# Selection rows by engine copies, normalisation also on POOL, halved last stores and more K transposes by DMA in an attention and gated-MLP kernel

## The chip, the cores and the metric

The kernel runs on one core of a Trainium2 chip. A core has five engines with an instruction stream each: TensorE (PE), VectorE (DVE), ScalarE (ACT), GpSimd (POOL) and SyncE (SP), which here only issues transfers. 16 DMA engines move data between HBM and the on-chip memory SBUF. TensorE writes its results to PSUM. The metric is the device time of one execution in microseconds (us); a smaller one is better.

## The reference

```
q, k, v: 4 batches x 8 heads x 768 positions x 64, float32
k_min, k_max = minimum and maximum of k over each chunk of 32 positions (24 chunks)
ub    = sum over d of max(q*k_min, q*k_max)          # a bound per query and chunk
top   = the 6 chunks with the largest bound, among those not after the query's
attn  = softmax(q k^T / 8, over keys in the top chunks and not after the query)
x     = attn v, heads side by side: 4 x 768 x 512
h     = gelu_tanh(x w_in);  u, g = halves of h (512 columns each)
g_n   = (g - mean) / sqrt(var + 1e-6) * g_ln
g_s   = w_sg g_n + b_sg                               # mixes the 768 positions
out   = x + (u * g_s) w_out
```

## The kernel before

*Units.* Two heads make a pair; there are 16 pairs `p`, four to a batch `b`. A pair goes through preparation, scores, and the product with v; after four pairs the MLP of that batch runs. A tag such as `sc_8_1_0` names one piece of work: the scores of pair 8, head 1, piece 0.

*Preparation.* q and k come in as rows and are transposed. For q (`qside`) TensorE transposes in float32 (`qtr`, L524), ScalarE or VectorE take the result out of PSUM (`qev`, L435/L438), a bf16 copy goes to the tile QA (`qcast`), and a copy without its negative part to rT (`rel`). For K there are two ways. Pairs below KD (`kside`): TensorE transposes (`ktr`, L524), VectorE takes minima and maxima by chunk (`kmm`, L563), evictions write the tile KA (`kev`). Pairs from KD on (`kside_full`): VectorE reduces k rows with a transposing reduction (`kred`, L580), TensorE puts the results in order (`perm`, L602) and VectorE copies them (`wcp`); a bf16 copy of k (`kcast`) is transposed into KA by a DMA transpose that SyncE issues (`kT`, L587). KD is 12.

*Selection.* TensorE forms the bounds (`ub`, L662 or L709); VectorE transposes them in blocks (`utr`), finds the sixth largest (`m8`), compares (`dn`) and transposes back (`dt`) into the tile Dt. From pair 4 on two pairs are selected together, and four transfers per two pairs (`qd`, L742, issued by SyncE) copy the rows of Dt into spare partitions of QA, 32 partitions by 576 columns each. The matching spare partitions of KA hold an indicator of chunks, so that one product over 128 partitions gives the score and a large negative number where the chunk was not selected.

*Scores and heads.* TensorE forms scores (`sc`, L778, and L818/L824 for pairs 0 to 3); ScalarE takes the exponential (`exp`, L784, L833); POOL clears what lies above the diagonal (`aff`, L789, L840). The product with v (`pv`, L856, and `pvd`, L863) also gives the sum; VectorE divides (`rcp`, `xs`, L871/L873) into XS.

*MLP of a batch.* XS is transposed, for batches 1 and 2 by DMA transposes (`dt_x`, L882), else on TensorE (`xtr`). Then `hv` (L905), its gelu (`gv`, L909) and statistics (`bns`, `bna`), the inverse root by a power on POOL (`rstd`, L920), and the normalisation of six row blocks (`vhat`, VectorE at L933 or ScalarE at L928). `hu` (L945) is the other half with its gelu (`gu`). `pt` (L962) mixes positions, VectorE multiplies (`vs`, `gt`), `ou` (L981) is the last product, VectorE adds x (`os`, L988) into one of three buffers osb, and SyncE stores it (`st`, L992).

*Order.* Nothing is scheduled at run time. The program builds a list of operations with their dependences; a table written into the kernel gives, for each engine, the order of its operations, the PSUM slot of each tile, an engine for operations that may run on several (`engine`), and the number of matmuls without use ahead of an operation of TensorE (`filler`). Each engine waits on semaphores for what its next instruction needs, and everything behind it in its order waits too. Before, 9 of 156 SyncE operations in the table's order are shown here, from the part in which batch 1's MLP begins:

```
kn_12 st_0_4 kn_11_0 kn_10_0 dt_x_1_0 dt_x_1_1 qd_8_1 dt_x_1_2 dt_x_1_3
```

Of the kernel before, what the change touches and what calls it, by code (L numbers as in the profile page):

```python
# [6 lines left out]
ALU = mybir.AluOpType  # L7
# [225 lines left out]
def dve(n, over=70, rate=1.0):  # L233
    o = n / rate / 0.96 + over
    return o, o + 83
# [22 lines left out]
def dmac(issue=530):  # L258
    return issue, issue


def _build(nc, ctx, q, k, v, w_in, g_ln, w_sg, b_sg, w_out, out):
# [49 lines left out]
    KD = 12  # L312
# [181 lines left out]
    QRUN = [0] * 16  # L494
    KRUN = [0] * 16
# [80 lines left out]
    def kside_full(p, u, x):  # L576
# [7 lines left out]
        for i in range(2):  # L584
            flex("pool", ("act",), lambda i=i: kbx[n][:, i, :, 64 * i:64 * i + 64], lambda i=i: kn[s][:, i], TG + 60,
                 ("kcast", p, i), [("kn", s, 0), ("kn", s, 1), ("kbi", n, i)], [("kbx", n, i)])
            P.op("sp", lambda e, i=i: e.dma_start_transpose(  # L587
                KA[w][i][:].rearrange("p (t x) -> p t x", x=128), kbx[n][:, i].rearrange("p t c -> p (t c)")), dmac(1250),
                ("kT", p, i), reads=[("kbx", n, i), ("kbi", n, i)], writes=[("KA", w, i, 0), ("KA", w, i, 1), ("KI", w, i)],
                dma=f"kT{w}_{i}", xfer=900)  # L590
# [102 lines left out]
    def select_full(pairs, u, v_):  # L693
# [45 lines left out]
        for x, p in enumerate(pairs):  # L739
            for i in range(2):  # L740
                w, g0 = p % NW, 32 * (2 * (1 - i) + x)
                P.op("sp", lambda e, w=w, i=i, g0=g0: e.dma_start(  # L742
                    QA[w][i][g0:g0 + 32, LO:S], Dt[v_][g0:g0 + 32].rearrange("p a b -> p (a b)")), dmac(590),
                    ("qd", p, i), reads=[("Dt", v_)], writes=[("QD", w, i)], dma=f"qd{w}_{i}", xfer=150)
# [133 lines left out]
    def xtrans(b, dk):  # L878
        src = XS[:, b % 2, dk]
        rd = [("XS", b % 2, 2 * dk), ("XS", b % 2, 2 * dk + 1)]  # L880
        if (b, dk) in DXT:
            P.op("sp", lambda e: e.dma_start_transpose(xT[b % 2][:, dk, :].rearrange("p (t x) -> p t x", x=128),  # L882
# [13 lines left out]
    def moe_h(b):  # L896
# [28 lines left out]
        for qt in range(NT):  # L925
# [6 lines left out]
            else:  # L932
                o = P.op("dve", lambda d, qt=qt: d.tensor_scalar(vhat[s][:, qt, :], vg[qt], mv[s][:, qt, 0:1],  # L933
                                                                 rstd[s][:, qt:qt + 1], op0=ALU.subtract,
                                                                 op1=ALU.mult),
                         (456, 548), ("vhat", b, qt), port=True,
                         reads=[("vg", qt), ("mv", s, qt), ("nmr", s), ("rstd", s)], writes=[("vhat", s, qt)])
            o.alts = {"act": (704, 809), "dve": (456, 548)}
# [15 lines left out]
    def moe_g(b):  # L954
        s = b % 2
        for tg in range(2):
# [19 lines left out]
            for qt in range(3 * tg, 3 * tg + 3):  # L976
                t = ps_g.tile((2, 3) if b < B - 1 else None)

                def ou(e, t=t, qt=qt):
# [7 lines left out]
                os_ = (b * NT + qt) % 3  # L987
                P.op("dve", lambda d, t=t, qt=qt, os_=os_: d.tensor_tensor(  # L988
                    osb[os_][:].rearrange("p (a x) -> p a x", x=128),
                    t.ap()[:, 0:DM].rearrange("p (a x) -> p a x", x=128), XS[:, b % 2, :, qt, :], op=ALU.add), dve(DM), ("os", b, qt),  # L990
                    reads=[t] + [("XS", b % 2, hh) for hh in range(H)], writes=[("osb", os_)], ps=[t])
                P.op("sp", lambda e, qt=qt, os_=os_: e.dma_start(  # L992
                    bass.AP(out.tensor, (b * S + 128 * qt) * DM, [[DM, 128], [1, DM]]), osb[os_][:]), dmac(),
                    ("st", b, qt), reads=[("osb", os_)], dma=f"o{os_}", xfer=680)
# [52 lines left out]
    for p in range(4, NP + 4):  # L1047
# [37 lines left out]
    "act": (  # L1085
# [10 lines left out]
    "dve": (  # L1096
# [106 lines left out]
```

## Time and profile before

| | |
|---|---|
| three runs | 219.81 us median, 219.38 to 221.41 |
| profiled execution | 220.97 us, span 219.1 us, mean granted TensorE clock 0.982 |
| busy | PE 205.8, DVE 185.9, ACT 169.5, POOL 93.2 us |
| DMA | 35.48 MB in 95067 packets, 162 GB/s mean |
| 24 `qd` transfers | 36 KB each, landing after a median 2.6 us |

The span is the time from the first to the last instruction of the trace. An engine is busy while it has an instruction in work; matmuls overlap, and a busy TensorE need not be at its peak. The granted clock is the share of TensorE's full clock. A row of a group of instructions names line, engine, operation, output and inputs, shapes and count, then the busy time in us, the mean ns of one, and the idle time of its engine just before with what ended it. A row of the chain of waits or of the timeline begins with its start and its length in us. PEld is TensorE's weight load, and SPq the issue of a transfer by SyncE.

### The profile page before, as it was taken

How to read it: one execution, taken by the hardware profiler on the slowest of the kernel's cores; microseconds unless marked ns; L12 is line 12 of the kernel's file. 1: busy time of each engine (PE TensorE's matmuls, PEld its weight loads, DVE VectorE, ACT ScalarE, POOL GpSimd, SP SyncE). 2: the span in 40 equal slices, each digit the busy share in tenths (PEclk: the TensorE clock that was granted, in tenths of full speed). 3: DMA queues.
4: the chain of work that ended last, by engine and by line, in shares of the span. 5: the costliest groups of instructions: out<-in, count | busy, mean ns of one | idle time of the engine just before them, and what ended most of it. 6: DMA issues, size and time to landing. Idle time of an engine off the chain costs nothing.

```text
span 219.1 us, 5967 instructions
## 1 busy us (share of the span) xinstructions
PE 205.8 (94%) x2357; PEld 134.1 (61%) x2357; DVE 185.9 (85%) x536; ACT 169.5 (77%) x256; POOL 93.2 (43%) x130
## 2 busy tenths in 40 slices
PE   7799999999999999997998989998799999999991
PEld 3477777846767577783355666776545669545640
DVE  3889999799999999998799987985896876968982
ACT  3778999979899899998668888998768978575000
POOL 8434699894374556464023537185102414002000
PEclk9879999999999999998899999999999999999999
DMA  7999999993999988947999849642955004000325
GB/s 153 249 219 205 223 211 375 294 237 124 248 225 238 208 231 200 225 81 135 263 233 179 141 81 224 75 113 56 217 105 124 0 0 146 3 0 0 144 87 201
DMA packets 95067, 35.48 MB, mean 162 GB/s; under 512 B 89280, under 2 KB 90048, under 8 KB 95040
## 3 DMA queue, kind: packets, MB, share of 16 engines
q1 hardware_dynamic: 95040, 35.11, 72.6%
q8 instruction: 18, 0.29, 0.6%
q14 instruction: 9, 0.07, 0.1%
HBM read 24.77 MB, written 6.29 MB: 142 GB/s over the span
## 4 chain that ended last, share of the span: by engine, by line
PE 63%; DVE 16%; ACT 11%; DMA 4%; issue 3%; SPq 0%; DVEq 0%
PE PSG L962 11%; PE PSG L945 7%; PE PSG L905 7%; PE PSC L778 7%; PE PSG L524 6%; ACT E L784 5%; PE PSG L856 4%; PE PSG L981 4%; DMA QA<-Dt 4%; DVE osb L988 3%; PE PSG L709 3%; PE PSC L818 3%; PE PSG L662 3%; DVE Wall L563 2%; DVE U L718 2%
## 5 line engine op out<-in xcount | busy, mean ns | idle before, releaser
L784 ACT ACTIVATE E<-PSC 128x1024 bf16<-128x1024 f32 (+1 forms) x72 | 63.4, 916 | 8.2 <-PE PSC L778 7.0
L778 PE MATMUL PSC<-QA,KA 128*128 128x128 bf16 (+2 forms) x336 | 37.2, 246 | 2.2 <-ACT E L784 1.2
L962 PE MATMUL PSG<-wsgT,vhat 128*128 128x384 bf16 x192 | 35.3, 326 | 0.6 <-DVE vhat L933 0.6
L789 POOL TENSOR_SCALAR_AFFINE_SELECT E<-E 128x768 bf16<-128x768 bf16 x24 | 21.1, 885 | 30.6 <-ACT E L784 30.2
L778 PEld LDWEIGHTS PSC<-QA,KA 128*128 128x128 bf16 x336 | 24.3, 98 | 12.6 <-ACT E L784 3.2
L438 POOL CAST QA<-qT 64x768 bf16<-64x768 f32 (+1 forms) x24 | 20.6, 860 | 22.1 <-ACT qT L435 13.4
L905 PE MATMUL PSG<-winb,xT 128*128 128x512 bf16 x96 | 24.4, 397 | 1.8 <-DVE XS L873 1.1
L962 PEld LDWEIGHTS PSG<-wsgT,vhat 128*128 128x128 bf16 x192 | 17.8, 98 | 11.8 <-ACT qT L435 1.0
L563 DVE TENSOR_REDUCE Wall<-PSG 128x12 f32<-128x384 f32 x48 | 24.7, 540 | 0.3 <-PE PSG L524 0.2
L945 PE MATMUL PSG<-xT,winb 128*128 128x384 bf16 x128 | 24.4, 327 | 0.0
L950 ACT ACTIVATE uT<-PSG 128x384 bf16<-128x384 f32 x32 | 15.5, 490 | 11.3 <-PE PSG L945 10.6
L981 PE MATMUL PSG<-woutb,uT 128*128 128x512 bf16 x96 | 23.7, 379 | 0.0
L909 ACT ACTIVATE vgb<-PSG 128x512 f32<-128x512 f32 x24 | 14.3, 598 | 11.0 <-PE PSG L905 10.9
L968 DVE SCALAR_TENSOR_TENSOR PSG<-PSG,glnT,bsgbc 128x384 f32<-128x384 f32 x32 | 19.5, 618 | 2.4 <-PE PSG L962 2.3
L920 POOL TENSOR_TENSOR rstd<-rstd,neghalf 128x6 f32<-128x6 f32 x4 | 5.3, 1330 | 37.5 <-DVE rstd L918 37.5
L833 ACT ACTIVATE E<-PSC 128x1024 bf16<-128x1024 f32 (+1 forms) x24 | 20.7, 918 | 0.2
L856 PE MATMUL PSG<-vx,E 128*128 128x65 bf16 x480 | 19.9, 194 | 0.4 <-DVE osb L988 0.3
L988 DVE TENSOR_TENSOR osb<-PSG,XS 128x512 f32<-128x512 f32 x24 | 16.0, 683 | 5.0 <-PE PSG L981 4.0
L914 DVE BATCH_NORM_STATS2 stats<-vgb 128x6 f32<-128x512 f32 x24 | 16.2, 681 | 3.2 <-ACT vgb L909 3.0
L856 PEld LDWEIGHTS PSG<-vx,E 128*128 128x128 bf16 x480 | 17.3, 98 | 2.3 <-DVE osb L988 0.6
L873 DVE TENSOR_TENSOR XS<-PSG,rden 128x384 bf16<-128x384 f32 x32 | 17.6, 554 | 0.6
L972 DVE TENSOR_TENSOR uT<-PSG,uT 128x384 bf16<-128x384 f32 x32 | 17.3, 550 | 0.5
(106 smaller groups left out, 370.8 us busy)
## 6 DMA issues: line engine op xcount, KB each, us to landing
qn<-in_q_dram SPq DMA_DIRECT2D x32, 192.0 KB, 4.5
vn<-in_v_dram SPq DMA_DIRECT2D x16, 384.0 KB, 5.5
out_dram<-osb SPq DMA_DIRECT2D x24, 256.0 KB, 2.7
kn<-in_k_dram SPq DMA_DIRECT2D x24, 192.0 KB, 4.6
uT<-in_moe_w_sg_dram SPq DMA_DIRECT2D x4, 384.0 KB, 5.8
vgb<-in_moe_w_in_dram SPq DMA_DIRECT2D x3, 512.0 KB, 9.1
kn<-in_k_dram SPq DMA_DIRECT2D x4, 384.0 KB, 4.5
QA<-Dt SPq DMA_DIRECT2D x24, 36.0 KB, 2.6
```

The lines of the kernel that those rows point to most:

```text
L438: return e.tensor_copy(dst(), src())
L563: P.op("dve", lambda d, m=m, op=op, t=t, hf=hf: d.tensor_reduce(W[w][:, m, 12 * hf:12 * hf + 12], t.ap()[:, 0:TG].rearrange("p (c x) -> p ...
L778: r = e.matmul(t.ap()[:, o:o + n], KA[w][i][:, 128 * kb:128 * kb + 128], QA[w][i][:, q0:q0 + n], start=True, stop=True)
L784: P.op("act", lambda e, t=t, c0=c0, c1=c1, i=i: e.activation(E[es][:, i, c0:c1], t.ap()[:, 0:c1 - c0], ACTF.Exp, scale=SCALE), act(c1 - c0 ...
L789: P.op("pool", lambda g, ev=ev: g.affine_select(ev, ev, pattern=[[0, NT], [1, 128]], compare_op=ALU.is_ge, fill=0.0, base=0, channel_multi ...
L833: P.op("act", lambda e, t=t, c0=c0, c1=c1, n=n: e.activation(E[es][:, :, c0:c1], t.ap().rearrange("p (i x) -> p i x", i=2)[:, :, 0:n], ACT ...
L856: r = e.matmul(t.ap()[:, 65 * qb:65 * qb + 65], E[es][:, i, a:a + 128], vx[w][:, kb, i, :], start=first, stop=False, skip_group_check=True)
L905: r = e.matmul(t.ap()[:, 0:F], xT[s][:, dk, 128 * qt:128 * qt + 128], winb[:, dk, F:DFF], start=(dk == 0), stop=(dk == NDK - 1))
L945: r = e.matmul(t.ap()[:, 0:TG], winb[:, dk, 128 * fb:128 * fb + 128], xT[s][:, dk, TG * tg:TG * tg + TG], start=(dk == 0), stop=(dk == NDK ...
L962: r = e.matmul(t.ap()[:, 0:TG], vhat[s][:, sb, 128 * fb:128 * fb + 128], wsgT[:, sb, TG * tg:TG * tg + TG], start=(sb == 0), stop=(sb == N ...
L981: r = e.matmul(t.ap()[:, 0:DM], gT[s][:, fb, 128 * qt:128 * qt + 128], woutb[:, fb, :], start=(fb == 0), stop=(fb == NF - 1))
L988: P.op("dve", lambda d, t=t, qt=qt, os_=os_: d.tensor_tensor(osb[os_][:].rearrange("p (a x) -> p a x", x=128), t.ap()[:, 0:DM].rearrange(" ...
```

## The change

1. KD goes from 12 to 10: pairs 10 and 11 take the second way for K.
2. The `qd` copies become operations that the table may give to POOL, VectorE or ScalarE: 16, 4 and 4. They are marked `shift`, by which POOL waits for the instruction before it on POOL and the next one waits for it.
3. `vhat` may also run on POOL. By batch, POOL takes 4, 5, 0 and 1, VectorE 0, 0, 6 and 4, ScalarE 2, 1, 0 and 1.
4. The last three row blocks of the output are added and stored in halves, into the q buffers instead of osb; their stores may be issued by ScalarE (three of six are).
5. DMA transposes may be issued by another engine by the table; here all stay on SyncE.
6. The table is new: all five orders, the slots, the fillers (12 matmuls at three places; before, 8 at one) and the engines of other operations.

```diff
-    KD = 12
+    KD = 10
...
-                P.op("sp", lambda e, w=w, i=i, g0=g0: e.dma_start(
-                    QA[w][i][g0:g0 + 32, LO:S], Dt[v_][g0:g0 + 32].rearrange("p a b -> p (a b)")), dmac(590),
-                    ("qd", p, i), reads=[("Dt", v_)], writes=[("QD", w, i)], dma=f"qd{w}_{i}", xfer=150)
+                flex("pool", ("dve", "act"), lambda w=w, i=i, g0=g0: QA[w][i][g0:g0 + 32, LO:S],
+                     lambda g0=g0: Dt[v_][g0:g0 + 32].rearrange("p a b -> p (a b)"), NSEL, ("qd", p, i), [("Dt", v_)],
+                     [("QD", w, i)], shift=True)
...
-                o = P.op("dve", lambda d, qt=qt: d.tensor_scalar(vhat[s][:, qt, :], vg[qt], mv[s][:, qt, 0:1],
+                o = P.op(eng, lambda d, qt=qt: d.tensor_scalar(vhat[s][:, qt, :], vg[qt], mv[s][:, qt, 0:1],
...
+                last, os_ = b == B - 1 and qt > 2, (b * NT + qt) % 3
+                dst = qn[os_][:].rearrange("p i t d -> p (i t d)")[:, 0:DM] if last else osb[os_][:]
...
+                for c0, c1 in ((0, DM // 2), (DM // 2, DM)) if last else ((0, DM),):
...
     "filler": (
-        "50:8 "),
+        "49:8 58:2 83:2 "),
```

In the new order of SyncE, the part in which batch 1's MLP begins reads:

```
kn_12 dt_x_1_0 kT_10_1 dt_x_1_1 kT_10_0 dt_x_1_2 dt_x_1_3 qn_13_0 qn_13_1
```

On TensorE, between the product with v of pair 7 and the first `hv` of batch 1, the orders are:

```
before: pvd_7_1 ktr_11_1 sc_8_1_2 sc_8_1_0 ktr_10_0 sc_8_1_1 ktr_10_1 hv_1_1
after:  pvd_7_1 qtr_11_0 qtr_12_0 sc_8_1_0 sc_8_1_2 ub_10 sc_8_1_1 qtr_12_1 hv_1_1
```

More of the change, by code (lines that the diff above doesn't have):

```diff
@@ L494, in _build @@
     QRUN = [0] * 16
+    TENG = "sp"
     KRUN = [0] * 16
@@ L586, in kside_full @@
                  ("kcast", p, i), [("kn", s, 0), ("kn", s, 1), ("kbi", n, i)], [("kbx", n, i)])
-            P.op("sp", lambda e, i=i: e.dma_start_transpose(
+            P.op(ENG.get(f"kT_{p}_{i}", TENG), lambda e, i=i: e.dma_start_transpose(
                 KA[w][i][:].rearrange("p (t x) -> p t x", x=128), kbx[n][:, i].rearrange("p t c -> p (t c)")), dmac(1250),
@@ L881, in xtrans @@
         if (b, dk) in DXT:
-            P.op("sp", lambda e: e.dma_start_transpose(xT[b % 2][:, dk, :].rearrange("p (t x) -> p t x", x=128),
+            P.op(ENG.get(f"dt_x_{b}_{dk}", TENG), lambda e: e.dma_start_transpose(xT[b % 2][:, dk, :].rearrange("p (t x) -> p t x", x=128),
                                                        src.rearrange("p t c -> p (t c)")), dmac(1250), ("dt_x", b, dk),
@@ L932, in moe_h @@
             else:
[L933 to L936, printed above, removed]
+                o = P.op(eng, lambda d, qt=qt: d.tensor_scalar(vhat[s][:, qt, :], vg[qt], mv[s][:, qt, 0:1],
+                                                               rstd[s][:, qt:qt + 1], op0=ALU.subtract,
+                                                               op1=ALU.mult),
+                         (456, 548) if eng == "dve" else (590, 640), ("vhat", b, qt), port=True,
                          reads=[("vg", qt), ("mv", s, qt), ("nmr", s), ("rstd", s)], writes=[("vhat", s, qt)])
-            o.alts = {"act": (704, 809), "dve": (456, 548)}
+            o.alts = {"act": (704, 809), "dve": (456, 548), "pool": (590, 640)}
         for fb in range(NF):
@@ L986, in moe_g @@
                      writes=[t], alloc=t)
[L987 to L994, printed above, removed]
+                last, os_ = b == B - 1 and qt > 2, (b * NT + qt) % 3
+                dst = qn[os_][:].rearrange("p i t d -> p (i t d)")[:, 0:DM] if last else osb[os_][:]
+                names = [("qn", os_, 0), ("qn", os_, 1)] if last else [("osb", os_)]
+                for c0, c1 in ((0, DM // 2), (DM // 2, DM)) if last else ((0, DM),):
+                    P.op("dve", lambda d, t=t, qt=qt, dst=dst, c0=c0, c1=c1: d.tensor_tensor(
+                        dst[:, c0:c1].rearrange("p (a x) -> p a x", x=128),
+                        t.ap()[:, c0:c1].rearrange("p (a x) -> p a x", x=128), XS[:, b % 2, c0 // 128:c1 // 128, qt, :],
+                        op=ALU.add), dve(c1 - c0), ("os", b, qt) + ((c0,) if last else ()),
+                        reads=[t] + [("XS", b % 2, hh) for hh in range(c0 // 64, c1 // 64)],
+                        writes=names if not last else [("qn", os_, c0 // 256)], ps=[t])
+                    tag = ("st", b, qt) + ((c0,) if last else ())
+                    o = P.op(ENG.get("_".join(str(x) for x in tag), "sp"), lambda e, qt=qt, dst=dst, c0=c0, c1=c1: e.dma_start(
+                        bass.AP(out.tensor, (b * S + 128 * qt) * DM + c0, [[DM, 128], [1, c1 - c0]]), dst[:, c0:c1]), dmac(),
+                        tag, reads=names if not last else [("qn", os_, c0 // 256)],
+                        dma=f"o{os_ + 3 * last}_{c0}", xfer=680 if not last else 360)
+                    if b == B - 1:
+                        o.alts = {"sp": (610, 610), "act": (571, 571)}
     SEL, GRP, UB, u = {}, {}, {}, 0
@@ L1069 @@
     "pe": (
[15 rows of a table removed]
-    "act": (
[10 rows of a table removed]
-    "dve": (
[17 rows of a table removed]
-    "pool": (
[12 rows of a table removed]
[15 rows of a table added]
+    "act": (
[10 rows of a table added]
+    "dve": (
[17 rows of a table added]
+    "pool": (
[13 rows of a table added]
     "slots": (
-        "12031220301320010101111100132013100110321002010100132121110011001023001011001013201010102333222223332333"
-        "33332222223211100133101001001022110001110100230100111000320111012323333322322332222223232233101110331010"
-        "01002310011011011132100110002301101023233232322233233233232323220110112311100012210100112301000012310113"
-        "312201300011200212333031"),
+        "21032331201202300101000110120130101010320131000011123130110110001132101000101013200110113223322323322322"
+        "22232332332310000132111101001132000010001001230111100132011010323232332332223222323333232310111023110100"
+        "11220101010110103201001101230101102323323332222323323233232332100101230111001221100000230100110231100212"
+        "2301200133213102100321"),
     "filler": (
-        "50:8 "),
+        "49:8 58:2 83:2 "),
     "engine": (
[8 rows of a table removed]
[10 rows of a table added]
 }
```

125 rows, old and new, of the table TABLE are left out of this document.

## The prediction

> **What bounds the kernel now.** I read the page's busy times first, then TensorE's own list of waits, then tables of stretches for the granted clock, and last the chain of waits around the worst stretch.
>
> ```profile
> span 219.1 us, 5967 instructions
> PE 205.8 (94%) x2357; PEld 134.1 (61%) x2357; DVE 185.9 (85%) x536; ACT 169.5 (77%) x256; POOL 93.2 (43%) x130
> ```
>
> TensorE is the bound as a sum: 13.3 us of the span without a matmul, part of that the start and the tail. POOL has the room. The next view names all that TensorE visibly waited for (engine, line, releaser: us in total, times, longest):
>
> ```profile
> PE PSC L778 <- ACT E L784: 1.2, 2, 0.7
> PE PSG L905 <- DVE XS L873: 1.1, 1, 1.1
> PE PSC L778 <- DMA QA<-Dt: 0.9, 2, 0.6
> PE PSG L905 <- DMA xT<-XS: 0.6, 1, 0.6
> PE PSG L962 <- DVE vhat L933: 0.6, 1, 0.6
> PE PSG L524 <- ACT KA L435: 0.4, 1, 0.4
> ```
>
> No wait is long. What makes them dear is the clock; the columns after the stretch are its length, then busy us of PE, PEld, DVE, ACT and POOL, the granted clock, DMA share and GB/s:
>
> ```profile
> 6.42:9.83 3.41, 1.82 (x18) 1.15 (x21) 3.33 (x9) 3.15 (x7) 1.37 (x4) 1.00 1.27 243
> 9.83:13.24 3.41, 3.41 (x26) 2.16 (x19) 2.54 (x15) 1.08 (x3) 0.00 (x0) 0.50 1.30 245
> 98.58:101.99 3.41, 1.86 (x12) 0.92 (x12) 3.41 (x7) 3.37 (x6) 2.54 (x4) 1.00 0.62 70
> 101.99:105.40 3.41, 3.07 (x10) 0.91 (x8) 1.62 (x4) 2.00 (x3) 0.00 (x0) 0.50 1.08 241
> 50.00:100.00 50.00, 48.77 (x556) 35.28 (x554) 48.33 (x139) 46.98 (x79) 27.61 (x35) 1.00 0.91 194
> ```
>
> Twice a stretch in which TensorE was busy 1.8 to 1.9 us of 3.41 is followed by one at half clock. The last row says that from 50 to 100 us VectorE has only 1.67 us free, so there it is a second bound. Around the second dip the timeline of TensorE and the chain of waits show what was late:
>
> ```profile
> 99.45 0.61 PE L778 MATMUL PSC<-QA,KA 128*128 128x384 bf16 x4 [0.50 <-ACT E L784]
> 100.46 0.55 PE L524 MATMUL PSG<-identF,kn 128*128 128x128 f32 x3 [0.39 <-ACT KA L435]
> 101.65 0.74 PE L905 MATMUL PSG<-winb,xT 128*128 128x512 bf16 x2 [0.65 <-DMA xT<-XS]
> ...
> 100.46 0.56 PE PSG L524 x3
> 101.18 3.97 DMA QA<-Dt
> 105.28 0.65 PE PSC L778 x7
> ```
>
> So the K transposes of pair 10 wait for the evictions of pair 11 (`kev`), `hv` of batch 1 waits for the transposed x, and the scores of pair 8 for its selection rows, which left the SyncE queue at 101.18 behind two transposes and a load and landed 3.97 us later.
>
> **The change part by part, against 219.1 us of span.** The profiled execution took 220.97 us, 1.87 more than its span and 1.16 above the 219.81 median of the runs; I take differences from the span and apply them to the median.
>
> *K side of pairs 10 and 11* (KD 12 to 10). Rows for what goes and what comes:
>
> ```profile
> L563 DVE TENSOR_REDUCE Wall<-PSG 128x12 f32<-128x384 f32 x48 | 24.7, 540 | 0.3 <-PE PSG L524 0.2
> L580 DVE TRANSPOSE_TENSOR_REDUCE Bn<-kn 128x24 f32<-128x768 f32 x8 | 7.6, 964 | 1.8 <-DMA kn<-in_k_dram 1.8
> L435 ACT ACTIVATE KA<-PSG 64x384 bf16<-64x384 f32 x24 | 11.6, 482 | 0.3
> 118.97 0.32 PE PSG L602 x27
> 98.40 0.32 PEld L524 LDWEIGHTS PSG<-identF,kn 128*128 128x128 f32 x3 [0.30 <-ACT KA L435]
> ```
>
> TensorE loses four groups of three transposes. A group costs between the 0.32 us of its weight loads and the 0.56 us of the chain piece, which includes the drain; followed by other matmuls it is nearest the former: 4 x 0.35 = 1.4. One permutation group (0.32) is added: -1.1 us of TensorE time, bounds -0.9 and -1.9. VectorE loses 8 reductions (4.3) and gains 4 of the transposing kind (3.9); ScalarE has 11 evictions fewer (5.3 us), while VectorE has 3 more over the whole kernel. These lie beside TensorE and are not counted here. Four DMA transposes are added on SyncE's queue; the copies that leave it (below) more than make room.
>
> *Selection rows* (`qd`). 24 transfers leave SyncE; 16 copies go to POOL, 4 to ScalarE, 4 to VectorE.
>
> ```profile
> L742 SPq DMA_DIRECT2D QA<-Dt x24: 513/589/1077, 52.7 to 165.3; - x24
> DMA to landing us min/median/max: 1.8/2.6/5.3
> L438 POOL COPY KA<-INDF 64x768 bf16<-64x768 bf16 x8 | 6.6, 823 | 0.3
> L437 DVE TENSOR_SCALAR rT<-qT 128x576 f32<-128x576 f32 x5 | 2.8, 566 | 0.0
> ```
>
> A POOL copy of 576 columns is 576/768 of 823 = 0.62 us, so 9.9 us on an engine with 126 free; on VectorE at most 0.57 each, 2.3 in all. The latency from finished rows to scores falls from 0.59 + 2.6 or more to about 0.7, or 1.4 for the second pair. POOL works in order, so `qd` can stand behind a triangle mask (`aff`) or a cast, and the affine selects behind `qd` feed `pvd`; about 0.9 us at most each time.
>
> *What that is worth at 98 to 105 us.* The waits there are 0.50 + 0.39 + 0.65, and 0.3 of the 0.9 for QA: 1.9. The stretch at half clock holds 3.07 us of matmul time, half of it lost: 1.5. Together 3.4. One wait stays: `hv_1` still needs the last transposed x.
>
> ```profile
> L882 SPq DMA_TRANSPOSE xT<-XS x8: 1211/1270/2305, 89.6 to 151.7; - x8
> DMA to landing us min/median/max: 2.7/3.2/5.5
> 96.30 4.20 SPq L882 DMA_TRANSPOSE xT<-XS  x2
> 200.40 0.65 PE PSG L945 x4
> 151.50 1.21 PE PSG L709 x32
> L873 DVE TENSOR_TENSOR XS<-PSG,rden 128x384 bf16<-128x384 f32 x32 | 17.6, 554 | 0.6
> ```
>
> From the end of pair 7's `pvd`, normalising (0.55 and a reciprocal, together an estimated 0.8) and landing (3.2) make 4.0 us. In the new order three q transpose groups (0.35 each), the bounds of pair 10 (1.1 of the 1.21 us piece) and three score blocks (a third of a microsecond each without their drain, an estimate from the 0.65 us pieces) stand in that place: 3.2 us, against three groups and three blocks, some 2.1, before. 0.8 us of wait remains, a little more than now, but a 3.41 us window with 2.6 busy is more than the 1.86 after which the clock fell: Taking 0.7 off the 3.4 for it, I take -2.7, bounds 0 (the wait is only renamed and the clock still falls) and -3.4. Elsewhere the QA wait at pair 12 goes: -0.6, bounds 0 and -0.6.
>
> The Trainium skill (TensorE: Matmul & The Clock Gate, Part 1: The HAM clock gate) lays the half clock to an idle window of about 3.4 us. By that rule the 0.65 us waits would not cause it, the 1.5 us would not come back and the sum would be 217.5; the trace disagrees, since the clock fell behind a window with 1.86 us of matmuls.
>
> *Normalisation* (`vhat`). VectorE falls from 19 to 10, ScalarE from 5 to 4, POOL takes 10: four in batch 0, five in batch 1, one in batch 3.
>
> ```profile
> L933 DVE TENSOR_SCALAR vhat<-vgb,mv,rstd 128x512 bf16<-128x512 f32 x19 | 9.5, 566 | 0.1
> L438 POOL CAST woutb<-osb 128x512 bf16<-128x512 f32 x1 | 0.6, 611 | 2.3 <-DMA osb<-in_moe_w_out_dram 2.3
> L920 POOL TENSOR_TENSOR rstd<-rstd,neghalf 128x6 f32<-128x6 f32 x4 | 5.3, 1330 | 37.5 <-DVE rstd L918 37.5
> ```
>
> No row shows this operation on POOL. From below there is a cast of the same tile, 0.611; from above the only arithmetic on POOL, a power at 1.33. One streamed input and one output make it nearest the cast: 0.65. Batch 1 then needs 5 x 0.65 = 3.3 us after `nmr` instead of 4 x 0.566 = 2.3 on VectorE; the cover is the eight `hu` groups (0.65 each) plus four transpose groups, 6.6 us behind the last `hv`, against some 7 us of statistics, power and `vhat`. Term: 0, with the 0.6 us wait for `vhat` left as it is; without the cover, +1.0. VectorE's sum over the whole kernel falls by about 1 us only, since evictions and copies fill what `vhat` leaves.
>
> *First half.* Counting VectorE's instructions up to the normalisation of pair 7: two evictions of K for pair 4 or 5, two for pairs 6 and 7, one x eviction, one q eviction, four transposing reductions, two small copies and one `qd` more, six `vhat`, two reductions and two w_sg evictions fewer: about +2.5 us at the quoted means. The 1.67 us free in the quoted stretch, and what is free before it, must take it. I charge +1.0, bounds 0 and +2.8 (the surplus is largest at `dt_4`). Against it stand four more filler matmuls (12, not 8) where the first dip arose; the half-clock stretch cost at most 1.7, and other engines pace it too: -0.5, bounds 0 and -1.7.
>
> *Tail.* The last three row blocks are written in halves into buffers of their own, half of the stores issued by ScalarE.
>
> ```profile
> 213.69 1.03 PE L981 MATMUL PSG<-woutb,uT 128*128 128x512 bf16 x4
> 214.46 1.29 DVE L988 TENSOR_TENSOR osb<-PSG,XS 128x512 f32<-128x512 f32 x2 [0.50 <-DMA out_dram<-osb]
> out_dram<-osb SPq DMA_DIRECT2D x24, 256.0 KB, 2.7
> ```
>
> The 0.50 us wait for a buffer put the last addition 0.35 late; that goes. The last store carries 128 KB; between the 2.6 of 36 KB and the 2.7 of 256 KB little is to be had by medians, so 0.35 for it, which is the addition's second half running beside the first half's store. Term: -0.7, bounds 0 (ScalarE's issue costs SyncE's 0.59 once more) and -1.2.
>
> *New waits.* All five orders are rewritten, and TensorE already shows unrelated waits of 0.5 to 1.1 us; I charge one of average size, +0.8, bounds 0 and +3. Sum: -1.1 - 2.7 - 0.6 + 0 + 1.0 - 0.5 - 0.7 + 0.8 = **-3.8**, so 219.8 - 3.8 = **216.0 us** (217.2 for an execution like the profiled one).
>
> **Rivals.** *Hidden anyway* (0.18). TensorE's direct waits for QA are only 0.9 us, which speaks for it; if the stretch at 100 us refills with the wait for transposed x and the clock still falls, -1.1 and -0.7 remain: 218.0. Against it: the chain of waits runs 3.97 us through that transfer.
>
> *POOL becomes the bound of the normalisation: slower* (0.16). Place: between the power and `pt` in batches 0 and 1, POOL's nine `vhat` in a row, with masks and casts queued behind. At 1.33 us each they take 12.0, where VectorE took 10 x 0.566 = 5.7 (six in batch 0, four in batch 1): +6.3, and 222.3 us. Break-even is (5.7 + 3.8)/9 = 1.06 us each. For it: POOL's only arithmetic row. Against: the cast. The Trainium skill (GPSIMD Engine Reference, Performance versus the Vector engine) calls POOL the wrong place for elementwise work, VectorE being about twice as fast; twice 0.566 is 1.13, and by that rule the time would be 216.0 + 10.2 - 5.7 = 220.5; no row here shows that operation on POOL.
>
> *VectorE paces the first half* (0.10). Its 2.8 us surplus is not absorbed, `hv_1` comes late and the clock dips as before: -1.1 - 0.7 + 2.8 + 0.8 = +1.8, 221.6. For it: 48.33 us busy of 50. Against: its total falls.
>
> **How the numbers follow.** My forecast has 0.56. One per cent is what a measurement of this kernel can tell, 217.6 and 222.0 being the lines. Faster: 0.54 of the forecast and 0.04 of the hidden case, 0.58. Within: 0.02 of the forecast, 0.12 hidden, 0.02 POOL, 0.06 VectorE, 0.22. Slower: 0.14 POOL, 0.02 hidden, 0.04 VectorE, 0.20. The likeliest's own range is 213.3 to 217.8, from the bounds of the stage at 100 us and the new waits. The range given, 212.8 to 221.6, takes in the hidden and VectorE cases and the low end of POOL's; about 0.18 is left out.
>
> **What would show it.** Right: no half-clock stretch near 100 us, no QA wait on TensorE, `hv_1` two microseconds earlier, POOL `vhat` near 0.65 and `qd` near 0.62 us, POOL busy about 110 us, the last addition 0.8 us behind the last matmul. Wrong: `vhat` on POOL above 1 us with TensorE waiting for it at L962, a new wait of 2 us or more, or a dip that only moved.

## The result, and the profile after

The changed kernel took 230.41 us in the median (229.26 to 232.0, 4 runs), the kernel before 220.36 us beside it (219.38 to 221.41): ratio 1.046, interval 1.038 to 1.054. Ratios, here and below, leave out executions that lie over 1.5% above the quickest of their kernel, while medians and extremes take them all. It is slower by some ten microseconds, where 216.0 us was forecast and 212.8 to 221.6 was the range. The first rows of the profiled execution's page, then its groups of POOL and the waits of TensorE (engine, line, what ended the wait; us in total, times, longest):

```profile
span 228.3 us, 5988 instructions
PE 205.7 (90%) x2367; PEld 133.0 (58%) x2381; DVE 186.5 (82%) x535; ACT 167.2 (73%) x250; POOL 121.9 (53%) x157
```

```profile
L934 POOL TENSOR_SCALAR vhat<-vgb,mv,rstd 128x512 bf16<-128x512 f32 x10 | 20.9, 2103 | 1.3 <-DVE nmr L923 1.3
...
L438 POOL COPY QA<-Dt 32x576 bf16<-32x576 bf16 x16 | 10.5, 658 | 11.6 <-DVE Dt L738 7.2 <-DVE mv L917 3.7
```

```profile
PE PSG L963 <- POOL vhat L934: 12.7, 2, 7.4
PE PSC L359 <- DVE vhat L356: 1.2, 1, 1.2
PE PSG L525 <- DVE qT L438: 0.8, 1, 0.8
```

The busy times of the engines hardly moved: TensorE 205.7 us against 205.8, VectorE 186.5 against 185.9. The span grew by 9.2 us, and so did TensorE's idle time; the waits that are new have one releaser. TensorE waits twice for `vhat` on POOL, 12.7 us in all, longest 7.4; no other wait of it is over 1.2 us, and none for QA is left. The ten `vhat` took 2.10 us each, 3.7 times VectorE's 566 ns. The next row shows that the `qd` copies came out nearly as forecast, 0.658 us where 0.62 had been worked out.

The timeline of POOL and of TensorE at the two places (start, length, what ended the idle time before):

```profile
57.82 8.25 POOL L934 TENSOR_SCALAR vhat<-vgb,mv,rstd 128x512 bf16<-128x512 f32 x4 [0.49 <-DVE nmr L923]
...
118.56 10.30 POOL L934 TENSOR_SCALAR vhat<-vgb,mv,rstd 128x512 bf16<-128x512 f32 x5 [0.30 <-DVE nmr L923]
```

```profile
66.22 2.08 PE L963 MATMUL PSG<-wsgT,vhat 128*128 128x384 bf16 x6 [5.37 <-POOL vhat L934]
...
129.01 2.40 PE L963 MATMUL PSG<-wsgT,vhat 128*128 128x384 bf16 x7 [7.35 <-POOL vhat L934]
```

Batch 0's four run from 57.82 to 66.07 and TensorE's first `pt` starts at 66.22; batch 1's five run from 118.56 to 128.86 and `pt` starts at 129.01. In the kernel before, `pt` of the two batches starts at 60.4 and 117.8:

```profile
60.40 2.11 PE L962 MATMUL PSG<-wsgT,vhat 128*128 128x384 bf16 x12
...
117.84 1.14 PE L962 MATMUL PSG<-wsgT,vhat 128*128 128x384 bf16 x6 [0.60 <-DVE vhat L933]
```

The waits then cost a second time, through the clock. Stretches of the span (length, busy time of PE, PEld, DVE, ACT, POOL, then the granted clock):

```profile
59.80:63.20 3.40, 1.04 (x11) 0.62 (x9) 1.86 (x5) 3.36 (x6) 3.40 (x3) 1.00 0.80 169
...
61.40:64.80 3.40, 0.00 (x0) 0.00 (x0) 0.28 (x2) 3.30 (x4) 3.40 (x3) 0.77 0.70 163
63.20:70.00 6.80, 3.78 (x14) 2.50 (x15) 1.57 (x3) 2.02 (x3) 6.68 (x9) 0.50 0.85 179
124.60:134.90 10.30, 5.89 (x51) 2.89 (x52) 2.78 (x7) 1.78 (x3) 7.34 (x7) 0.50 0.01 1
```

The clock falls while TensorE still waits, and is at half for 6.8 us at the first wait and for 10.3 at the second. The matmul time in these stretches, 3.78 and 5.89 us, would have been half as long at full clock, by an estimate from these two figures: 4.8 us lost. All four executions show a mean granted clock of 0.96 to 0.97. Neither of the two dips of the kernel before is there. Waits and clock together are 17.5 us for 9.2 of span. The difference isn't attributed piece by piece: without these waits the changed kernel would have been the quicker one (e1), and while TensorE stood still the other engines went on, so that its other waits are at most 1.2 us. The row 61.40:64.80 answers another question as well: VectorE is busy 0.28 us in it while POOL's `vhat` go on at 2.06 each, so it isn't a contest of the two engines that makes them slow.

### The profile page after: what moved, and what is told of

Same layout as the page of the kernel before. It is cut to its first block, busy times and chain, and to the rows that moved or that the text cites. A ratio compares the mean times of both kernels' runs of the same rounds, so it can differ in the third digit from the quotient of the medians.

```text
span 228.3 us, 5988 instructions
## 1 busy us (share of the span) xinstructions
PE 205.7 (90%) x2367; PEld 133.0 (58%) x2381; DVE 186.5 (82%) x535; ACT 167.2 (73%) x250; POOL 121.9 (53%) x157
## 4 chain that ended last, share of the span: by engine, by line
PE 58%; DVE 23%; POOL 8%; ACT 7%; issue 3%; DVEq 0%
PE PSG L963 15%; POOL vhat L934 8%; PE PSC L779 8%; PE PSG L982 7%; PE PSG L946 5%; PE PSG L857 5%; PE PSG L525 5%; PE PSG L906 4%; DVE Wall L564 3%; DVE stats L915 3%; ACT E L785 3%; DVE Bn L581 2%; DVE XS L874 2%; DVE m L730 2%; PE PSC L359 2%
## 5 line engine op out<-in xcount | busy, mean ns | idle before, releaser
L963 PE MATMUL PSG<-wsgT,vhat 128*128 128x384 bf16 x192 | 38.2, 350 | 12.7 <-POOL vhat L934 12.7
L963 PEld LDWEIGHTS PSG<-wsgT,vhat 128*128 128x128 bf16 x192 | 19.1, 104 | 25.8 <-issue 16.2
L438 POOL CAST QA<-qT 64x768 bf16<-64x768 f32 (+1 forms) x23 | 19.4, 843 | 8.7 <-ACT qT L435 6.9
L564 DVE TENSOR_REDUCE Wall<-PSG 128x12 f32<-128x384 f32 x40 | 20.6, 545 | 3.2 <-PE PSG L525 2.9
L906 PE MATMUL PSG<-winb,xT 128*128 128x512 bf16 x91 | 22.1, 379 | 0.8 <-ACT vgb L910 0.3
L982 PE MATMUL PSG<-woutb,uT 128*128 128x512 bf16 x87 | 21.7, 379 | 0.7 <-POOL woutb L438 0.3
L934 POOL TENSOR_SCALAR vhat<-vgb,mv,rstd 128x512 bf16<-128x512 f32 x10 | 20.9, 2103 | 1.3 <-DVE nmr L923 1.3
L857 PEld LDWEIGHTS PSG<-vx,E 128*128 128x128 bf16 x480 | 17.5, 98 | 4.4 <-issue 1.4
L951 ACT ACTIVATE uT<-PSG 128x384 bf16<-128x384 f32 x32 | 14.9, 489 | 3.8 <-PE PSG L946 3.5
L946 PEld LDWEIGHTS PSG<-xT,winb 128*128 128x128 bf16 x128 | 11.4, 98 | 10.1 <-ACT uT L951 2.6
```

The lines of the kernel that those rows point to most:

```text
L564: P.op("dve", lambda d, m=m, op=op, t=t, hf=hf: d.tensor_reduce(W[w][:, m, 12 * hf:12 * hf + 12], t.ap()[:, 0:TG].rearrange("p (c x) -> p ...
L857: r = e.matmul(t.ap()[:, 65 * qb:65 * qb + 65], E[es][:, i, a:a + 128], vx[w][:, kb, i, :], start=first, stop=False, skip_group_check=True)
L906: r = e.matmul(t.ap()[:, 0:F], xT[s][:, dk, 128 * qt:128 * qt + 128], winb[:, dk, F:DFF], start=(dk == 0), stop=(dk == NDK - 1))
L934: o = P.op(eng, lambda d, qt=qt: d.tensor_scalar(vhat[s][:, qt, :], vg[qt], mv[s][:, qt, 0:1], rstd[s][:, qt:qt + 1], op0=ALU.subtract, op ...
L946: r = e.matmul(t.ap()[:, 0:TG], winb[:, dk, 128 * fb:128 * fb + 128], xT[s][:, dk, TG * tg:TG * tg + TG], start=(dk == 0), stop=(dk == NDK ...
L963: r = e.matmul(t.ap()[:, 0:TG], vhat[s][:, sb, 128 * fb:128 * fb + 128], wsgT[:, sb, TG * tg:TG * tg + TG], start=(sb == 0), stop=(sb == N ...
```

## The experiments

All are compared with the kernel before on the same chip; the ratio's interval is at 95%. A profile shows one execution; that of e1 is its slowest, 218.99 us, 1.0 above the median, so that differences of a microsecond between its trace and another's can be the execution's. The theory was that the price of one operation on POOL accounts for all of the loss; the rivals were that the new orders do, and that VectorE paces the first half.

**e1: `vhat` off POOL.** The changed kernel, with one thing undone.

```diff
-  vhat_0_4:pool vhat_0_5:pool vhat_0_0:pool vhat_0_1:pool vhat_1_4:pool ... vhat_3_2:pool
+  vhat_0_4:dve vhat_0_5:dve vhat_0_0:dve vhat_0_1:dve vhat_1_4:dve ... vhat_3_2:dve
...
+        for b, qts in ((0, (4, 5, 0, 1)), (1, (4, 0, 3, 5, 1)), (3, (2,))):
+            for qt in reversed(qts):
+                move(f"vhat_{b}_{qt}", "pool", "dve", f"nmr_{b}")
```

> The changed kernel with its ten POOL normalisations (vhat) moved to VectorE, right behind nmr of their batch; all else as changed. Theory P: POOL's vhat at 2.1 us each is the whole slowdown; the two TensorE waits of 5.4 and 7.4 us and the 17 us at half clock go, no vhat wait above 1 us stays, and the time is 216 us (213.5 to 218), below before. Rival F: other parts of the change (the rewritten orders, VectorE's surplus in the first half, selection copies in POOL's queue) cost several us too: 221 us or more. In between, 218 to 221, P holds for the slowdown and the rest of the change is worth nothing.

217.98 us in the median (217.31 to 218.99, 12 runs), ratio 0.992 (0.989 to 0.995). From 230.41 to 217.98 are 12.4 us: the whole loss, and more, hung on these ten instructions. Busy times and four stretches of e1:

```profile
PE 201.3 (93%) x2367; PEld 130.9 (60%) x2381; DVE 191.1 (88%) x545; ACT 167.3 (77%) x250; POOL 101.2 (47%) x147
```

```profile
20.00:50.00 30.00, 29.21 (x512) 20.88 (x513) 27.36 (x87) 27.91 (x41) 24.41 (x32) 1.00 1.04 265
50.00:80.00 30.00, 28.16 (x229) 18.44 (x229) 29.38 (x87) 26.17 (x45) 14.85 (x21) 1.00 1.00 209
80.00:100.00 20.00, 18.98 (x334) 14.27 (x335) 19.65 (x60) 18.64 (x31) 13.97 (x19) 1.00 0.81 160
100.00:120.00 20.00, 17.12 (x167) 9.83 (x165) 19.27 (x55) 17.49 (x30) 8.88 (x12) 1.00 1.20 207
```

The clock stays full from 4.6 to 216.3 us. With the same 2367 matmuls TensorE is busy 4.4 us less than in the changed kernel (201.3 for 205.7), which is about what the half clock was reckoned to cost; the busy time that had hardly moved there hid it. Of the 11.0 us between the two spans (228.3 and 217.3) the other 6.6 are TensorE's idle time. But VectorE now has 191.1 us of work where it had 185.9 before, and is busy 68.30 of the 70 us from 50 to 120. That may be a second ceiling, seen only once the first is gone; e5, e7 and e9 ask whether it is.

**e2: the same price in the kernel before.** The kernel before, with batch 1's four `vhat` of VectorE on POOL, behind the power; nothing else is changed.

```diff
-                o = P.op("dve", lambda d, qt=qt: d.tensor_scalar(vhat[s][:, qt, :], vg[qt], mv[s][:, qt, 0:1],
+                o = P.op(eng, lambda d, qt=qt: d.tensor_scalar(vhat[s][:, qt, :], vg[qt], mv[s][:, qt, 0:1],
...
+        for qt in (0, 4, 1, 3):
+            move(f"vhat_1_{qt}", "dve", "pool", "rstd_1")
```

> The kernel before with one thing changed: the four normalisations that VectorE does in batch 1 run on POOL, behind its power; the two on ScalarE stay. Theory P: 4 x 2.1 = 8.4 us in the place of 2.4 us, some 5 to 6 us of new TensorE wait ahead of pt of batch 1, then half clock for one or two stretches of 3.4 us: 4 to 8 us slower, 224 to 228 us. Rival F (POOL's vhat only hurts together with the new order): under 222 us, with a wait below 2 us.

226.92 us (225.07 to 231.29), ratio 1.032 (1.024 to 1.039). The timeline of POOL and the longest wait of TensorE in e2:

```profile
113.09 8.26 POOL L933 TENSOR_SCALAR vhat<-vgb,mv,rstd 128x512 bf16<-128x512 f32 x4 [0.47 <-DVE nmr L922]
```

```profile
PE PSG L962 <- POOL vhat L933: 5.8, 1, 5.8
```

8.26/4 is 2.07 us each and the wait is 5.8 us, with the old orders but for these four operations and none of the other edits. It is the operation, not its surroundings.

**e3: what in the operation is dear.** e1 with eight POOL instructions appended, when POOL has nothing else left to do; they write to buffers that nothing reads any more.

```diff
+            ("two_ap", lambda g: g.tensor_scalar(probe, src[:, 0:512], a, m, op0=ALU.subtract, op1=ALU.mult)),
+            ("one_ap", lambda g: g.tensor_scalar(probe, src[:, 0:512], m, None, op0=ALU.mult)),
+            ("two_imm", lambda g: g.tensor_scalar(probe, src[:, 0:512], 0.5, 2.0, op0=ALU.subtract, op1=ALU.mult)),
+            ("one_imm", lambda g: g.tensor_scalar(probe, src[:, 0:512], 2.0, None, op0=ALU.mult)),
+            ("half", lambda g: g.tensor_scalar(probe[:, 0:256], src[:, 0:256], a, m, op0=ALU.subtract, op1=ALU.mult)),
+            ("copy", lambda g: g.tensor_copy(pw, src[:, 0:512])),
+            ("bf16", lambda g: g.tensor_scalar(probe, pw, a, m, op0=ALU.subtract, op1=ALU.mult)),
+            ("tt", lambda g: g.tensor_tensor(probe, src[:, 0:512], src[:, 0:512], op=ALU.mult)),
```

> The kernel of e1 with eight POOL instructions appended to POOL's order, on dead tiles, for their durations: vhat's own form (512 columns, float32 to bf16, subtract and multiply, both scalars from SBUF), one scalar from SBUF, two constants, one constant, 256 columns, a copy, bf16 input, and tensor times tensor. If reading scalars from SBUF is dear: 2.1, about 1.3, 0.65, 0.65, then 1.1, 0.6, 2.1. If each arithmetic step is dear whatever the scalar: 2.1, 1.1 to 1.3, 2.1, 1.1 to 1.3. If it is contention with VectorE: all vary, and the copy is above 0.61 us. A fixed cost shows as the 256-column form well above half. Tensor times tensor about 1.1 to 1.4. The run's time says nothing beyond about 1 us.

219.46 us in a single execution. Each form runs once. The timeline of POOL near the end of e3, in the order of the diff:

```profile
196.20 2.28 POOL L1079 TENSOR_SCALAR KA<-vn,mv,rstd 128x512 bf16<-128x512 f32 x1
198.58 1.61 POOL L1080 TENSOR_SCALAR KA<-vn,rstd 128x512 bf16<-128x512 f32 x1
200.28 1.98 POOL L1081 TENSOR_SCALAR KA<-vn 128x512 bf16<-128x512 f32 x1
202.35 1.50 POOL L1082 TENSOR_SCALAR KA<-vn 128x512 bf16<-128x512 f32 x1
203.95 1.23 POOL L1083 TENSOR_SCALAR KA<-vn,mv,rstd 128x256 bf16<-128x256 f32 x1
205.25 0.61 POOL L1084 CAST KA<-vn 128x512 bf16<-128x512 f32 x1
205.97 2.07 POOL L1085 TENSOR_SCALAR KA<-KA,mv,rstd 128x512 bf16<-128x512 bf16 x1
208.12 1.04 POOL L1086 TENSOR_TENSOR KA<-vn 128x512 bf16<-128x512 f32 x1
```

On the same tile, a copy takes 0.61 us, a product of two tensors 1.04, one step with a scalar 1.50 to 1.61, two steps 1.98 to 2.28. It matters little whether the scalar is a number or a column in memory (1.98 for 2.28, 1.50 for 1.61), or whether the input is bf16 (2.07); half the columns take 1.23, a little over half. So the price lies in the form of the instruction, nearly in proportion to its length. The copy's 0.61, as in the kernel before, speaks against contention with VectorE here too. The forecast's nearest row, the cast, was the one form here that does no arithmetic.

By the Trainium skill (GPSIMD Engine Reference, Engine selection) POOL is about twice as slow as VectorE for two inputs, while one input runs at roughly line rate. The copy fits that, with 0.61 against the 0.566 of VectorE's `vhat`. For the product of two tensors VectorE's nearest row is its addition `os`, 0.68 on 128x512, which would make POOL 1.5 times as slow. `vhat` on POOL, which has one input, does not fit: it is twice as dear as the form with two.

**e4: `qd` back to transfers.** e1 with the 24 `qd` issued by SyncE again, each placed where its rows are ready.

```diff
-                flex("pool", ("dve", "act"), lambda w=w, i=i, g0=g0: QA[w][i][g0:g0 + 32, LO:S],
+                P.op("sp", lambda e, w=w, i=i, g0=g0: e.dma_start(
...
+                move(f"qd_{x}", next(e for e in ENGINES if at[f"qd_{x}"] in order[e]), "sp", after)
```

> The kernel of e1 with the selection rows (qd) moved by 24 transfers on SyncE again, each group of four placed in SyncE's order right behind the operation that was issued there when its rows were ready. Theory: the copies are worth 2 us (1 to 4) over e1, and TensorE waits for QA from a transfer again. Rival (hidden anyway): within 0.7 us of e1. Third: SyncE's queue is now freer, so e4 is faster than e1 by what the copies load POOL and VectorE.

221.46 us (219.82 to 222.6), ratio 1.006 (1.003 to 1.010): 3.2 us over e1 by the ratios. Waits of TensorE and two stretches of e4:

```profile
PE PSC L779 <- DMA QA<-Dt: 3.0, 2, 2.5
PE PSG L603 <- DVE Bn L581: 1.4, 1, 1.4
```

```profile
100.10:103.50 3.40, 1.06 (x19) 0.82 (x15) 2.60 (x7) 1.13 (x3) 2.01 (x3) 1.00 0.88 80
...
103.50:106.90 3.40, 3.20 (x42) 1.74 (x42) 0.00 (x0) 2.11 (x3) 1.41 (x3) 0.50 0.45 96
```

The wait for QA is back, and so is the half clock behind it, 3.20 us of matmuls at half speed. It isn't this execution alone: 10 of e4's 12 show a mean granted clock of 0.992 or less, while all of e1's show 0.997 or more. The part of the change that the forecast thought most of does what was forecast. (The placing of the 24 issues in SyncE's order was mine; in another order the wait might be shorter.)

**e5 and e10: VectorE relieved.** e1 with the four `qd` of VectorE on POOL; run twice.

```diff
-  qd_5_0:dve ... qd_8_0:dve ... qd_11_0:dve ... qd_15_0:dve
+  qd_5_0:pool qd_8_0:pool qd_11_0:pool qd_15_0:pool
```

> The kernel of e1 (217.98 us, 0.992 of the kernel before), with the four qd copies that VectorE still makes (L438 QA<-Dt 32x576, 0.53 us each by e1's groups) moved to POOL, where such a copy takes 0.65 us. Nothing else is moved. Theory A: VectorE paces the first 120 us of e1 (49.04 of 50 us busy from 50 to 100 us), so of the 2.1 us taken off it, 1.6 before 105 us, 1 to 2 come back: 216.0 to 217.0 us, ratio 0.983 to 0.987, with VectorE's busy time in the stretch from 50 to 100 us nearly unchanged and hv_1 earlier than 104.2. Rival B: the first half is held by the orders and by all engines in turn, and VectorE's full row is only its share of that: 217.5 to 218.5, ratio 0.990 to 0.994.

> e5 once more, beside e9 on one chip, for the comparison of the two: ratio 0.986 to 0.993, as it was.

218.4 us, ratio 0.989 (0.985 to 0.993), and then 218.16 us, ratio 0.994 (0.991 to 0.996). Between them lies e1's 0.992: the 2.1 us taken off VectorE bring nothing that can be measured. In the two profiled executions `hv_1` did start earlier, at 103.03 and 102.10 instead of 104.21, and the first `pt` of batch 1 at 118.66 and 117.96 instead of 118.82. In e5 most of the lead was gone by then: TensorE waited 1.97 us for Bn (the K side's reduction) until 118.22, and the clock fell behind that stretch, so that twelve matmuls of `pt` took 3.60 us, in e1 2.12.

```profile
114.90:118.30 3.40, 1.43 (x18) 0.70 (x19) 3.40 (x7) 3.36 (x7) 0.82 (x1) 1.00 1.09 241
```

```profile
118.22 0.51 PE L603 MATMUL PSG<-Bn,identF 64*32 64x24 f32 x32 [1.97 <-DVE Bn L581]
118.66 3.60 PE L963 MATMUL PSG<-wsgT,vhat 128*128 128x384 bf16 x12
```

Five of e5's 6 executions and five of e10's 12 have a mean clock of 0.992, e1's none. So a part of what the relief gave may have been lost again to the clock; how much isn't shown.

**e7: VectorE loaded.** The opposite of e5: two MAX8 without use ahead of each of the same four copies.

```diff
+            if eng == "dve" and tag[0] == "qd":
+                x = scr[tag[1]]
+                for c in range(2):
+                    e.max(x[0:32, c], src())
```

> The kernel of e1 with work added on VectorE: ahead of each of its four qd copies (about 54, 87, 100 and 150 us) two MAX8 over the same 32x576 numbers, with a result that nothing reads; an estimated 0.65 us each, so 5.2 us in all and 3.9 before 105 us. Theory A (VectorE paces the first 120 us): 3 to 5 us slower than e1, 221 to 223, ratio 1.005 to 1.015. Rival B (VectorE's full row is not what sets the end): 218 to 219.5.

221.98 us (220.91 to 223.07), ratio 1.007 (1.004 to 1.010), 3.3 us over e1 by the ratios. The group of what was added, 5.7 us of busy time:

```profile
L443 DVE MAX8 scr<-Dt 32x8 bf16<-32x576 bf16 x8 | 5.7, 742 | 0.1
```

The pairs ran at 54, 101, 130 and 174 us, the second and third later than the expectation put them: 2.84 us before 105 us, not 3.9 (nor the 4.5 that e9's expectation counts). Where they are paid for shows in TensorE's timeline, e7 first, then e1 (the first `pt` of batch 0, the first `hv` of batch 3):

```profile
62.01 1.14 PE L969 MATMUL PSG<-wsgT,vhat 128*128 128x384 bf16 x6
...
190.30 1.67 PE L912 MATMUL PSG<-winb,xT 128*128 128x512 bf16 x7
```

```profile
60.83 1.14 PE L963 MATMUL PSG<-wsgT,vhat 128*128 128x384 bf16 x6
...
187.49 1.67 PE L906 MATMUL PSG<-winb,xT 128*128 128x512 bf16 x7
```

The first pair, 1.42 us in batch 0's normalisation, makes `pt` 1.2 us late, nearly its whole length. `hv_1` and the first `hv` of batch 2 are 1.5 late each (105.70 for 104.21, 156.48 for 154.94), so the pairs at 101 and 130 us cost about 0.3 together. Another 0.5 comes by 162 us (`hu`, 162.72 for 160.68), ahead of the fourth pair, and 0.8 behind that pair, by 177 (a `pt` group at 177.45 for 174.59, with a wait of 0.66 for VectorE). VectorE thus paces the normalisation of batch 0 and a part of batch 2's MLP; its full row from 60 to 120 us doesn't mean that it sets the end there. Of the four copies that e5 took off it, those at 54 and 172 us stood where load is paid for, 0.70 and 0.31 us.

**e9: more relief.** e5 with four evictions of K near 60 us back on ScalarE, where the kernel before has them.

```diff
-  kev_7_0_0:dve kev_6_0_0:dve kev_7_1_1:dve kev_7_1_0:dve
+  kev_7_0_0:act kev_6_0_0:act kev_7_1_1:act kev_7_1_0:act
+        for x, after in (("7_0_0", "7_0_1"), ("6_0_0", "6_0_1"), ("7_1_1", "6_0_0"), ("7_1_0", "7_1_1")):
+            move(f"kev_{x}", "dve", "act", f"kev_{after}")
```

> The kernel of e5 (ratio 0.989 to the kernel before) with four more evictions of K taken off VectorE between 57 and 63 us (L438 KA<-PSG 64x384, 0.55 us each) and put on ScalarE, where the kernel before has them (0.49 us each). e7 showed that time added to VectorE in the first half is paid for (3.3 us for 4.5 us added before 105 us), e5 that 1.6 us taken off it bring 0.6 at most. Theory A (VectorE still paces the stretch around 60 us, where pt_0 waits for its vhat): 1 to 2 us less than e5, 216.0 to 217.2, ratio 0.980 to 0.985. Rival B (ScalarE, 45.5 of 50 us busy there, is now as tight, so that the exponentials of pairs 4 and 5 come later by what VectorE saves): no gain, ratio 0.988 to 0.996.

217.32 us (217.05 to 218.09), ratio 0.989 (0.986 to 0.993). Beside e10 on the same chip it is 0.4% less, about 0.9 us, and the two intervals overlap. The stretch from 50 to 100 us of e9:

```profile
50.00:100.00 50.00, 47.63 (x574) 33.17 (x583) 47.52 (x141) 47.18 (x80) 30.51 (x42) 1.00 0.94 194
```

VectorE has 47.52, ScalarE 47.18 and TensorE 47.63 of 50: three engines within half a microsecond. Relief of one can't be expected to bring much there. The first theory fails: the ratio is above its range, and in the traces e9's `pt_0` and `hv_1` start no earlier than e10's (60.50 and 102.45 for 60.07 and 102.10). The ratio lies in the rival's range; that the exponentials on ScalarE are what holds the stretch is not shown. With 0.989, e9 is the quickest version here, though e5's first run gave the same ratio.

**e6: fillers.** e1 with eight filler matmuls at one place, not twelve at three.

```diff
-        "49:8 58:2 83:2 "),
+        "49:8 "),
```

> The kernel of e1 with eight filler matmuls ahead of one instruction of TensorE only, the four at two later places left out. The prediction charged the fillers -0.5 us with bounds 0 and -1.7. Theory A: the stretch at half clock that the kernel before has from 9.8 to 13.2 us comes back, and the kernel takes 0.5 to 1.7 us more: 218.5 to 219.7. Rival B: the new order alone keeps the clock up there, or other engines pace that stretch: 217.6 to 218.4, with at most a short dip.

219.67 us (217.68 to 221.06), ratio 0.995 (0.991 to 0.998), which overlaps e1's. The profiled execution, 218.01 us, shows no early dip (granted clock 1.00 over the first 50 us) and is one of the three quickest of 12; the others lie at 219.3 and above and have no trace. But seven of these nine show a mean granted clock of 0.997 or more, so a dip, which would make it 0.992, isn't what sets them apart. It stays open whether the fillers are worth 0.7 us or nothing, and by what.

**e8: tail undone.** e1 with the last three blocks added and stored whole, through osb, all by SyncE.

```diff
-                for c0, c1 in ((0, DM // 2), (DM // 2, DM)) if last else ((0, DM),):
+                for c0, c1 in ((0, DM),) if last else ((0, DM),):
...
+                dst, names = osb[os_][:], [("osb", os_)]
```

> The kernel of e1 with the last three row blocks added and stored whole, through the three common buffers and with all stores by SyncE, as before the change. The prediction charged the halves -0.7 us, bounds 0 and -1.2. Theory A: 218.3 to 219.2, ratio about 0.995, with the last addition waiting again for a buffer. Rival B: worth nothing, 217.6 to 218.3, since ScalarE's issues cost what the shorter additions save.

220.7 us (219.92 to 221.66), ratio 1.000 (0.998 to 1.003): 1.9 us over e1 by the ratios, more than either theory said. The last additions and the stores, e8 first, then e1:

```profile
213.11 1.89 DVE L991 TENSOR_TENSOR osb<-PSG,XS 128x512 f32<-128x512 f32 x3 [1.92 <-PE PSG L982]
...
209.55 6.76 SPq L998 DMA_DIRECT2D out_dram<-osb  x6
```

```profile
211.72 2.48 DVE L992 TENSOR_TENSOR qn<-PSG,XS 128x256 f32<-128x256 f32 x6
...
212.50 1.73 ACTq L999 DMA_DIRECT2D out_dram<-qn  x3
```

In e8 the last three additions start together at 213.11, behind an idle 1.92 us; in e1 they follow one another from 211.72. The row names TensorE as releaser, but at TensorE's even pace from 207.67 to 212.81 us the fourth of six row blocks was finished by about 211.1; what was left to wait for is the buffer of the first block, whose store was issued at 209.55. That is read from the order and not shown by a row of its own; it fits that the DMA engines' mean busy share is 0.78 from 212.3 to 213.0 us and 0 from there to 213.7. e8 undoes halves, buffers and ScalarE's issues together, so it doesn't say which of them is worth how much.

## Why the prediction was wrong, step by step

*The step that failed is the price of `vhat` on POOL, and with it the term 0*: "One streamed input and one output make it nearest the cast: 0.65", with 1.33 as the bound from above. Measured: 2.10 us. With it the forecast's own formula for the rival that POOL becomes the bound gives 9 x 2.10 = 18.9, less 5.7 on VectorE: +13.2, so 216.0 + 13.2 = 229.2 us, against 230.41 measured. The rival's mechanism and its place (between the power and `pt` of batches 0 and 1) were right; it was given 0.16 because one price was wrong. Its break-even (1.06 us each) no run tests. That the formula comes within 1.2 us is partly luck: it charges each `vhat` in full and has no term for the clock, while the changed kernel had 12.7 us of waits and an estimated 4.8 from the clock, of which a part didn't reach the end. Both bounds were taken from rows of other operations, and "from above" was no bound: the power works on 6 columns, so its 1.33 us says nothing about 512. The nearest row by shape was a copy, 0.611; `vhat` came out 3.4 times as dear, and by e3 that is the price of its two arithmetic steps. The signs listed under "Wrong" came out as written: `vhat` above 1 us, TensorE waiting for it at that line, a new wait of over 2 us.

*Half clock.* That "the clock fell behind a window with 1.86 us of matmuls" was the forecast's reading, against the rule of an idle window in the Trainium skill (TensorE: Matmul & The Clock Gate, Part 1: The HAM clock gate). That reading held: in e4 it fell behind a window with 1.06 us busy, in the changed kernel behind 1.04. But the forecast used it only to book a gain, and did not ask what a long wait elsewhere would do by it: an estimated 4.8 us of matmul time here. Nor did it ask how common the two dips are that it booked at 1.5 and 0.5. The profiled execution has a mean clock of 0.982; of 65 others of the kernel before, which the ratios of e1 to e10 take in, 47 have 0.995 or more, where a single step of 3.4 us would leave 0.992. Their median is 219.8 us, that of the other 18 is 220.5. So in most executions there was no such dip to win back.

*`qd` and the stage at 100 us* (-2.7 and -0.6). Held: 3.2 us by e4, the price 0.658 for 0.62, no wait for QA, no half clock there. (The four waits it lists add to 1.84, not 1.9.) e4 is another order than the old one, though, so its 3.2 is the price of the transfers there, and the size before is not shown by itself. Only "`hv_1` two microseconds earlier" failed: in e1 it starts at 104.21, in the kernel before at 101.65. The work before it has become more, and the gain shows later: the first `hv` of batch 2 starts at 154.94 instead of 156.11.

*VectorE in the first half* (+1.0, bounds 0 and +2.8). In the changed kernel it could not be seen, since VectorE stood still for POOL. In e1 it has 97.82 us of work in the first 105, before 93.90: 3.9 more, for `vhat` is back while the evictions that had filled its place stayed. e7 shows that such time is paid for nearly in full around 55 us and hardly at 101 and 130, so a surplus has no one rate, and how much of the 2 us that separate e1 from the forecast is VectorE's stays open. Summing a surplus over half the kernel was the wrong way to price it; its place decides.

*Tail* (-0.7, bounds 0 and -1.2). Not settled in size: e8 gives 1.9, above the bound. From the last matmul to the end of the span it is 4.4 us in the kernel before (214.71 to 219.1) and 3.9 in e1 (213.40 to 217.3), so against the old tail as it was the gain is nearer 0.5; e8's stores met a longer wait for a buffer than the old kernel's 0.41 and 0.50.

*K side* (-1.1) was not tried alone. *Fillers* (-0.5): open, by e6. *New waits* (+0.8): in e1 TensorE has several of about 1 us, one of them 1.6 for Bn at pair 10; no sum of them is shown.

## What to carry to other kernels

Before an operation moves to another engine, find a row of that very form on that engine; where there is none, the price of a copy is not a bound, and a line appended at the end of a kernel measures it in one run. Ask of every move how much time there is until someone waits (here 4 and 5 instructions in a row before one matmul), and put into the loss the clock that falls behind a long wait. A dip that is to be won back should be looked for in several executions first. A full row of an engine doesn't say that it sets the end: the same load cost nearly its whole length at one place and next to nothing at two others.

## What the runs showed of the hardware

POOL's price depends on the form of the instruction far more than on its bytes: on 128x512 from 0.61 us (copy) to 2.28 (two scalar steps), and it hardly falls with a bf16 input (2.07) or with scalars given as numbers (1.98). The half clock lasts in whole steps of about 3.4 us: 3.4 in e4, 6.8 and 10.3 in the changed kernel. It does not need an idle TensorE. Stretches of that length that end where the clock falls, or would have (in e1 counted back in steps of 3.41 us from 216.2, where its clock falls after the last matmul), in the kernel before and in e1:

```profile
6.42:9.83 3.41, 1.82 (x18) 1.15 (x21) 3.33 (x9) 3.15 (x7) 1.37 (x4) 1.00 1.27 243
```

```profile
62.66:66.07 3.41, 2.16 (x14) 1.24 (x14) 3.34 (x8) 3.09 (x4) 2.57 (x5) 1.00 0.89 218
117.27:120.68 3.41, 2.20 (x44) 1.42 (x44) 3.41 (x6) 3.38 (x5) 0.01 (x1) 1.00 0.78 183
```

With 1.82 and, in the prediction's row, 1.86 us busy it fell, as it did with 1.43 in e5, 1.06 in e4 and 1.04 in the changed kernel; with 2.16 and 2.20 it stayed. One stretch of e9 (113.99 to 117.41) has 1.82 and kept its clock, so the line is not sharp in busy time, or the stretch was not cut where the chip cuts it.
